# A table of planned starts, annealed with longer transfers in the plan, in place of the search in an attention and mixing kernel

## The chip, the cores and the metric

One core of one Trainium2 chip runs the whole program; the other cores are not used. The metric is the device time of one execution in microseconds, as the median over runs. The kernel before takes 596.05 us, the median of 3 runs (595.01 to 597.22).

## The reference

The reference is causal attention in a window of 128 positions with a linear bias, and a mixing block over its result:

```python
scores = scale * np.matmul(q, k.transpose(0, 1, 3, 2))
scores = np.where(mask, scores + bias[None], -1000000000.0)
attn = np.exp(scores - np.max(scores, axis=-1, keepdims=True))
attn = attn / (np.sum(attn, axis=-1, keepdims=True) + 1e-09)
x = np.matmul(attn, v)                      # 8 batches, 8 heads, 576 rows, 64 columns
theta = x @ w_theta                         # x as 8 x 576 x 512
zr, zi = x * np.cos(theta), x * np.sin(theta)
y = np.einsum('ts,bsd->btd', w_tok_r, zr) + np.einsum('ts,bsd->btd', w_tok_i, zi)
u = x + y
out = u + np.maximum(u @ w_ch, 0.0)
```

## The kernel before

Heads are taken in pairs, 4 pairs to a batch and 32 in all. For a pair, TensorE (PE) makes the scores in two groups (L624); VectorE (DVE) adds the band and takes the least value of each row (L648); ScalarE (ACT) makes the exponentials (L653). From pair 7 on ("late" pairs) the weights are split into two halves of 16 bits, the high one on ACT (L673) and the low one on DVE (L675), and are turned by a DMA transpose that SyncE (SP) issues (L679); the turned tiles are `pta` to `ptd`. PE then multiplies them with the values (L699 and L704, 72 matmuls for a pair: "attend"), and DVE divides by the sums (L712 to L716).

When the 4 pairs of a batch are there, the batch is turned, also by DMA transposes (L866, L867, L871), multiplied with the angle weights (L803, 12 matmuls a block; L808 and L812 for the short block), and made into `z_hi` and `z_lo` by way of the sine table (L826 to L845 and L420). Then PE mixes the tokens (L917): 8 results a batch, each of 27 matmuls of 288 columns, done in three parts of 9. DVE adds each result to `xtf` (L923), ACT and DVE split it (L927, L930), and PE does the channels (L951, 12 matmuls each); ACT, POOL or DVE finish, and SP stores (L970). The two banks `m_psa` and `m_psb` carry the results of L917 and L951 in turns, so that a bank is free for the next result only when DVE or ACT has read it. At the start, the three weight matrices are loaded in chunks (L432), and unpacked and split by DVE and ACT (L436 to L491), among the work on the first pairs.

Every step is first only recorded, with a cost (`Plan.__call__`): its engine, how long the engine is held, and a delay until its result can be used. A DMA is two steps, one on SP for the issue, and one on an engine called "DMA", which does one transfer at a time. `Plan.order` then sets the order: it simulates the plan backward and forward several times with greedy choices, keeps the best, and moves the keys of the steps by a fixed list of random numbers, `NUDGES`. `Plan.run` emits the steps in the order found, so that each engine's queue is in that order, and no engine passes a step by. Where the plan sees PE free, `run` puts filler matmuls of 187 columns on a tile of ones (L376, `spin`): one for each 0.085 of planned gap before 130, and one for each 0.085 of 0.8 of the gap after it.

Of the kernel before, what the change touches and what calls it, by code (L numbers as in the profile page):

```python
# [52 lines left out]
while RAD * 0.5 > math.pi:  # L53
# [11 lines left out]
TABLE = 1.3  # L65
HOLD = 12.0
RETILE = 0.11
STAY = 1.0
# [3 lines left out]
ROUNDS = 6  # L72
SELF = {"DVE": 0.115, "ACT": 0.13, "POOL": 0.1}
NUDGES = (
# [11 lines left out]
)  # L86
# [45 lines left out]
class Plan:  # L132
# [47 lines left out]
    def simulate(self, key, back):  # L180

        steps = self.steps
        engines = ("PE", "DVE", "ACT", "POOL", "SP", "DMA")
        free = dict.fromkeys(engines, 0.0)
        held = {"DVE": 0.0, "POOL": 0.0}
        open_ = {e: [] for e in engines}
        events, start = [], [0.0] * len(steps)
        wait = [len(s.after if back else s.deps) for s in steps]
        ready = [0.0] * len(steps)
        for s in steps:  # L190
            if not wait[s.n]:
                heapq.heappush(events, (0.0, s.n))
        table, now, order, tiled = None, 0.0, [], "f"
        into, out_of = (1, 0) if back else (0, 1)
        while len(order) < len(steps):
            while events and events[0][0] <= now + 1e-9:
                n = heapq.heappop(events)[1]
                heapq.heappush(open_[steps[n].engine], (key[n], n))
            for e in engines:
                if free[e] > now + 1e-9 or not open_[e]:  # L200
                    continue
                if e == "ACT":
                    extra = lambda t: TABLE if t.table not in (None, table) else 0.0
                    weight = HOLD / TABLE
                elif e == "PE":
                    extra = lambda t: RETILE if t.modes[into] != tiled else 0.0
                    weight = STAY / RETILE
                else:
                    other = {"DVE": "POOL", "POOL": "DVE"}.get(e)
                    extra = lambda t: max(0.0, held[other] - now) if t.port else 0.0  # L210
                    weight = 1.0
                if e == "DMA" and not back:
                    best = min(open_[e], key=lambda x: (ready[x[1]], x[1]))
                else:
                    best = min(open_[e], key=lambda x: (x[0] + weight * extra(steps[x[1]]), x[1]))
                open_[e].remove(best)
                heapq.heapify(open_[e])
                s = steps[best[1]]
                free[e] = now + s.busy + extra(s)
                table = s.table or table  # L220
                if e == "PE":
                    tiled = s.modes[out_of]
                if s.port:
                    held[e] = free[e]
                start[s.n] = free[e] - s.busy
                order.append(s)
                for a in (s.deps if back else s.after):
                    t = steps[a]
                    late = SELF.get(e, 0.0) if t.engine == e else t.late if back else s.late
                    wait[a] -= 1  # L230
                    ready[a] = max(ready[a], free[e] + late)
                    if not wait[a]:
                        heapq.heappush(events, (ready[a], a))
            if len(order) < len(steps) and not (events and events[0][0] <= now + 1e-9):
                now = min([t for t in free.values() if t > now + 1e-9] + [max(e[0], now) for e in events[:1]])
        end = max(free.values())
        if back:
            start = [end - t - s.busy for t, s in zip(start, steps)]
        return end, order, start

    def nudge(self, key, first, seed, span):

        state = seed

        def draw():
            nonlocal state
            state = (state * 6364136223846793005 + 1442695040888963407) & (1 << 64) - 1
            return (state >> 11) / (1 << 53)

        draw(), draw()  # L250
        size = 10.0 * draw()
        size *= draw()
        middle, about = draw() * span, 5.0 + draw() * 100.0
        sparse = draw() < 1.0 / 3.0
        out = []
        for k, t in zip(key, first):
            up, chance = draw(), draw()
            out.append(k + size * (2.0 * up - 1.0) if abs(t - middle) < about and (not sparse or chance < 0.2) else k)
        return out

    def order(self):
        steps = self.steps
        ahead = [0.0] * len(steps)
        for s in steps:
            ahead[s.n] = max((ahead[d] + steps[d].busy + steps[d].late for d in s.deps), default=0.0)
        key, best, span = [-(t + s.busy) for t, s in zip(ahead, steps)], None, 700.0
        for _ in range(ROUNDS):
            _, _, last = self.simulate(key, True)
            end, order, first = self.simulate(last, False)
            if best is None or end < best[0]:  # L270
                best = end, order, first, last
            key = [-(t + s.busy) for t, s in zip(first, steps)]
        end, order, first, last = best
# [7 lines left out]
        for s, t in zip(steps, first):  # L281
            s.start = t
# [19 lines left out]
def attn_moe_kernel(ctx: ExitStack, tc: tile.TileContext, qt, kt, vx, wth, wtok, wch, band, out):  # L302
    nc = tc.nc
# [800 lines left out]
```

## Time and profile before

| | |
|---|---|
| median of 3 runs | 596.05 us |
| the profiled execution | 594.92 us |
| its span, first to last instruction | 593.1 us |
| mean granted clock of TensorE | 0.994 |
| PE busy, fillers included | 580.1 us, 98% |
| fillers (L376), busy | 71.5 us in 556 |
| DVE, ACT, POOL busy | 493.1, 475.1, 157.1 us |

The span is what the trace covers; 1.8 us of the execution lie around it. PE counts as busy during its fillers, so its 98% has to be read together with them. A matmul's busy time is its passage through the engine, and matmuls overlap: 9 mixing matmuls follow each other in 1.10 us although each is shown with 0.29 us.

### The profile page before, as it was taken

Reading aid. Unit: us, or ns where it says so; the run is one execution under the profiler, and the core shown is the slowest. Engines: PE = TensorE matmul, PEld = TensorE weight load, DVE = VectorE, ACT = ScalarE, POOL = GpSimd, SP = SyncE. Lnnn points to the kernel's source line nnn. Section 1 sums busy time; section 2 is a strip of 40 time slices with the busy share of each in tenths; the row PEclk is TensorE's granted clock in tenths of the full one; section 3 lists DMA queues with packets and bytes.
Section 4 is the critical chain, followed back from the end, with each engine's and each line's share of the span. In section 5 each row is a group of like instructions: output and inputs, shape, how many; then the busy total and the mean of one; then the engine's idle time right before and its main releaser. Section 6 shows DMA issues by size and latency. Waiting matters only on the chain.

```text
span 593.1 us, 18474 instructions
## 1 busy us (share of the span) xinstructions
PE 580.1 (98%) x7524; PEld 442.8 (75%) x7524; DVE 493.1 (83%) x1523; ACT 475.1 (80%) x902; POOL 157.1 (26%) x135
## 2 busy tenths in 40 slices
PE   8999999999998999999999989999999999999997
PEld 8888876886676677776776757786767676777776
DVE  5999999999896998799879988878977989865333
ACT  4999999787999999999788978985998766446213
POOL 0000120011663106610573004700280127106000
PEclk9999999999998999999999989999999999999999
DMA  8975640897876964985469666438362613201102
GB/s 309 408 305 193 182 103 10 181 203 176 186 167 120 203 165 96 190 209 134 67 154 244 144 112 155 90 107 178 64 117 79 116 38 96 56 11 41 41 1 81
DMA packets 140102, 82.03 MB, mean 138 GB/s; under 512 B 119152, under 2 KB 127600, under 8 KB 140016
## 3 DMA queue, kind: packets, MB, share of 16 engines
q1 hardware_dynamic: 140016, 80.84, 56.4%
q8 instruction: 59, 0.97, 0.7%
q14 instruction: 27, 0.22, 0.1%
HBM read 42.29 MB, written 9.44 MB: 87 GB/s over the span
## 4 chain that ended last, share of the span: by engine, by line
PE 77%; ACT 8%; DVE 7%; DMA 4%; issue 2%; POOL 1%; SPq 0%; ACTq 0%; POOLq 0%
PE m_psa L917 15%; PE m_psb L917 15%; PE m_psa L951 8%; PE m_psb L951 7%; PE s_ps L624 7%; PE t_psa L803 6%; PE t_psb L803 5%; PE a_psa L376 3%; PE a_psa L704 2%; PE a_psb L376 2%; PE a_psb L704 2%; PE a_psa L699 1%; DMA xpa<-hlxa 1%; DMA ptc<-hla 1%; DMA ptb<-hlb 1%
## 5 line engine op out<-in xcount | busy, mean ns | idle before, releaser
L917 PEld LDWEIGHTS <-z_hi 128*128 128x128 f16 x1152 | 111.8, 98 | 31.9 <-issue 2.2
L951 PEld LDWEIGHTS <-wch 128*128 128x128 f16 x780 | 75.2, 98 | 19.2
L917 PE MATMUL m_psb<-wtk_hi,z_hi 128*128 128x288 f16 x288 | 83.1, 289 | 2.0 <-DVE xtfb L923 2.0
L917 PE MATMUL m_psb<-wtk_hi,z_lo 128*128 128x288 f16 x288 | 83.2, 289 | 0.0
L917 PE MATMUL m_psb<-wtk_lo,z_hi 128*128 128x288 f16 x288 | 83.1, 288 | 0.0
L917 PE MATMUL m_psa<-wtk_hi,z_hi 128*128 128x288 f16 x288 | 82.4, 286 | 0.0
L917 PE MATMUL m_psa<-wtk_hi,z_lo 128*128 128x288 f16 x288 | 82.4, 286 | 0.0
L917 PE MATMUL m_psa<-wtk_lo,z_hi 128*128 128x288 f16 x288 | 82.4, 286 | 0.0
L917 PEld LDWEIGHTS <-z_lo 128*128 128x128 f16 x576 | 56.6, 98 | 14.5
L420 POOL TENSOR_TENSOR z_lo<-wch_held,z_hi 128x512 f16<-128x512 f32 x32 | 40.7, 1285 | 87.0 <-ACT z_hi L845 52.2
L376 PEld LDWEIGHTS <-white 128*128 128x128 bf16 x556 | 48.9, 100 | 13.0 <-issue 5.9
L951 PE MATMUL m_psa<-u,wch 128*128 128x288 f16 (+1 forms) x396 | 53.2, 284 | 0.0
L376 PE MATMUL a_psa<-white 128*128 128x187 bf16 x418 | 50.0, 250 | 1.7 <-DVE a_psa L389 1.5
L951 PE MATMUL m_psb<-u,wch 128*128 128x288 f16 (+1 forms) x384 | 51.5, 284 | 0.0
L867 POOL TENSOR_TENSOR hlxa<-x_sba,hlxa 128x512 f16<-128x512 f32 (+1 forms) x12 | 16.2, 1347 | 111.0 <-ACT hlxa L866 111.0
L653 ACT ACTIVATE sba<-sba,fixed 128x192 f32<-128x192 f32 x88 | 36.3, 448 | 5.2 <-DVE fixed L648 4.5
L653 ACT ACTIVATE sbb<-sbb,fixed 128x192 f32<-128x192 f32 x84 | 34.7, 448 | 4.6 <-DVE fixed L648 4.6
L653 ACT ACTIVATE sbc<-sbc,fixed 128x192 f32<-128x192 f32 x84 | 34.7, 446 | 3.9 <-DVE fixed L648 3.9
L927 ACT ACTIVATE u<-xtfb,fixed 128x288 f16<-128x288 f32 x32 | 16.5, 527 | 24.5 <-DVE xtfb L923 24.5
L803 PEld LDWEIGHTS <-xpb 128*128 128x128 f16 x192 | 18.5, 98 | 21.4 <-DMA xpb<-hlxb 1.4
L803 PEld LDWEIGHTS <-xpa 128*128 128x128 f16 x192 | 18.4, 98 | 20.4 <-DMA xpa<-hlxa 1.1
L648 DVE CUSTOM_DVE_ANT_0 sbb<-s_ps,bands 128x192 f32<-128x192 f32 x84 | 26.5, 346 | 7.8 <-PE s_ps L624 7.7
(420 smaller groups left out, 1613.0 us busy)
## 6 DMA issues: line engine op xcount, KB each, us to landing
vba<-in_vx_dram SPq DMA_DIRECT2D x6, 845.0 KB, 6.3
out_dram<-xtfa SPq DMA_DIRECT2D x32, 144.0 KB, 1.9
out_dram<-xtfb SPq DMA_DIRECT2D x31, 144.0 KB, 1.8
vbb<-in_vx_dram SPq DMA_DIRECT2D x5, 845.0 KB, 5.4
vbc<-in_vx_dram SPq DMA_DIRECT2D x5, 845.0 KB, 5.8
qra<-in_qt_dram SPq DMA_DIRECT2D x11, 288.0 KB, 3.9
kra<-in_kt_dram SPq DMA_DIRECT2D x11, 288.0 KB, 3.8
krb<-in_kt_dram SPq DMA_DIRECT2D x11, 288.0 KB, 3.8
```

The lines of the kernel that those rows point to most:

```text
L376: nc.tensor.matmul(spun, white[:, :128], white[:, :spun.shape[-1]], start=True, stop=True)
L420: plan(engine, cost, lambda: on.tensor_tensor(out=out, in0=whole, in1=part, op=ALU.subtract), r=r, w=w, port=True)
L624: nc.tensor.matmul(ps.tile[at:at + 64, e, to:to + kn], qr.tile[rows, q0:q0 + 64], kr.tile[rows, k0:k0 + kn], start=True, stop=True)
L648: plan("DVE", (0.08 + kn * 1.03e-3, 0.13), lambda: nc.vector.tensor_tensor_reduce(out=out, in0=source, in1=bands[:out.shape[0], h, at:at + ...
L653: plan("ACT", (0.187 + kn * 0.833e-3, 0.15), lambda: nc.scalar.activation(out, source, AF.Exp, bias=least, scale=-1.0), r=r, w=w, table="exp")
L699: nc.tensor.matmul(av[e][cols, i, :d], block(c_, 1, a)[rows, cols], v[rows, slot, :d], start=c == 0 and k == 0, stop=False, skip_group_che ...
L704: nc.tensor.matmul(av[e][:, c + 1, :d], block(c, 2 * e, a), v[:, 4 * e + c, :d], start=False, stop=k == len(products) - 1, skip_group_chec ...
L803: nc.tensor.matmul(t_ps, a[:, c * 128:c * 128 + 128], w[:, c, :], start=(k == 0 and c == 0), stop=(k == len(prods) - 1 and c == 3))
L867: plan("POOL", pool(512), lambda: nc.gpsimd.tensor_tensor(out=lo, in0=x, in1=hi, op=ALU.subtract), r=every + [(hlx, "h")], w=[(hlx, "l")])
L917: nc.tensor.matmul(y.tile[:, :HALF], z[:, c, m * 128:m * 128 + 128], w[:, c, cs], start=(part == 0 and j == 0 and a == 0), stop=(part == 2 ...
L927: plan("ACT", (0.43, 0.15), lambda m=m, cs=cs, at=at: nc.scalar.activation(u_hi[:, m, cs], at, AF.Copy, scale=share), r=[(xtf, ("y", m, hf ...
L951: nc.tensor.matmul(o.tile[:, :n], w[:, c, e * 128:e * 128 + 128], u[:, c, cs], start=(k == 0), stop=(k == 11))
```

## The change

`Plan.order` no longer searches. It reads a table `STARTS`, one planned start in hundredths for every step in the order of recording, and sorts the steps by it. The simulation, the nudging and their constants are gone. `run` is as it was, and computes its fillers from the table's starts. Seven costs of transfers are changed; each is (SP held, "DMA" engine held, delay). The instructions that compute are the same, in number and in kind; their order on every engine is another, and there are 497 fillers for 556. Lines of the same statement lie 54 further down in the changed kernel: L376 becomes L430, L624 L678, L699 L753, L917 L971, L923 L977.

```diff
+STARTS = """
+    0 70 110 344 330 428 372 358 414 386 400 194 398 152 298 404 990 482 1426 1440 1931 2122 2196 2238 2314 2333
...
+    56501 56543 56583 56621 56479 56579 56621 56661 56697
+"""
...
     def order(self):
...
+        starts = [int(t) for t in STARTS.split()]
+        assert len(starts) == len(self.steps)
+        for s, t in zip(self.steps, starts):
+            s.start = t / 100.0
+        return sorted(self.steps, key=lambda s: (s.start, s.n))
...
-        issued.append(plan("SP", (0.42, w * 2.55e-3 + (0.7 if len(issued) < 3 else 0.0), 2.15),
+        issued.append(plan("SP", (0.42, w * 2.85e-3, 1.25),
...
-        plan.follow(plan("SP", (0.4, 0.75, 2.05), lambda: nc.sync.dma_start(
+        plan.follow(plan("SP", (0.42, 1.0, 1.2), lambda: nc.sync.dma_start(
...
-        values_issue[g] = plan("SP", (0.42, 2.05, 2.3), lambda: nc.sync.dma_start(
+        values_issue[g] = plan("SP", (0.36, 2.9, 1.6), lambda: nc.sync.dma_start(
...
-            plan("SP", (1.9, 2.0, 0.0), lambda hl=hl, turned=turned: nc.sync.dma_start_transpose(
+            plan("SP", (1.44, 2.0, 0.4), lambda hl=hl, turned=turned: nc.sync.dma_start_transpose(
...
-            plan("SP", (1.3, 1.4, 0.5) if wide else (1.2, 0.75, 0.65), lambda: nc.sync.dma_start_transpose(
+            plan("SP", (1.24, 1.42, 0.5) if wide else (1.2, 0.77, 0.55), lambda: nc.sync.dma_start_transpose(
...
-        plan("SP", (0.34, 0.45, 1.3), lambda: nc.sync.dma_start(
+        plan("SP", (0.36, 0.52, 1.2), lambda: nc.sync.dma_start(
```

The first place is PE at the end of batch 2 and the start of batch 3, where pair 12 attends (`pta` and `ptb` are its turned weights, `krc`, `qrc` the keys and queries of pair 14). Before:

```order
L917 MATMUL m_psb<-wtk_hi,z_lo 128x288
L376 LDWEIGHTS white
L376 MATMUL a_psb<-white 128x187
...
L624 MATMUL s_ps<-krc,qrc 64x64 x2
L376 LDWEIGHTS white
L376 MATMUL a_psb<-white 128x187
...
L699 LDWEIGHTS pta
L699 MATMUL a_psa<-vhb,pta 64x65
```

In the changed kernel, from the same scores on:

```order
L678 MATMUL s_ps<-krc,qrc 64x64 x2
L430 LDWEIGHTS white
L430 MATMUL a_psb<-white 128x187
L971 LDWEIGHTS z_hi
L971 MATMUL m_psa<-wtk_hi,z_hi 128x288
...
L678 MATMUL s_ps<-kra,qra 64x64 x2
L753 LDWEIGHTS pta
L753 MATMUL a_psa<-vhb,pta 64x65
```

Before, 5 fillers, a group of scores and 10 fillers stood directly ahead of the attend, and 17 and 5 more followed. Now one filler follows the scores, then 36 mixing matmuls, another group of scores, 24 angle matmuls and a third group of scores, and only then pair 12 attends.

The second place is DVE ahead of its first addition of a mixing result (L923, now L977), in batch 0. Before:

```order
L420 TENSOR_TENSOR z_lo<-fga,z_hi 128x512
L648 ISA firstb,fixed<-s_ps,bands 64x64
L648 ISA fixed 64x1
L675 SCALAR_TENSOR_TENSOR hlb<-sba,hlb 128x768
L582 TENSOR_TENSOR fixed<-fixed 128x1
...
L648 ISA sba,fixed<-s_ps,bands 128x192
L648 ISA fixed 128x1
L923 SCALAR_TENSOR_TENSOR xtfa<-m_psb,fixed,xtfa 128x288
L715 RECIPROCAL fixed<-fixed 128x5
L531 TENSOR_REDUCE fixed<-vbb 128x1
```

And in the changed kernel:

```order
L474 TENSOR_TENSOR z_lo<-wch_held,z_hi 128x512
L769 RECIPROCAL fixed<-fixed 128x5 x2
L652 TENSOR_SCALAR fixed<-fixed 128x1
L770 TENSOR_TENSOR x_sbb<-a_psb,fixed 128x5x64
L770 TENSOR_TENSOR x_sbb<-a_psa,fixed 128x5x64
L662 SCALAR_TENSOR_TENSOR vla<-vba,fixed,vha 128x832
L729 SCALAR_TENSOR_TENSOR hlb<-sba,hlb 128x768
L977 SCALAR_TENSOR_TENSOR xtfa<-m_psb,fixed,xtfa 128x288
L585 TENSOR_REDUCE fixed<-vbc 128x1
L702 ISA sba,fixed<-s_ps,bands 128x192
```

More pairs are divided and more values split or measured ahead of the first addition, and fewer scores. Counted from the start of the queue, the changed kernel has one L531, one L608, two L716 and eight small instructions more there (by the old lines), and three pairs of L648 fewer.

The third place is PE at pair 24, whose second group of scores is made from `kra` and `qra` and which attends with `pta` and `ptb`. In the changed kernel:

```order
L678 MATMUL s_ps<-kra,qra 64x128
...
L430 LDWEIGHTS white
L430 MATMUL a_psa<-white 128x187
...
L678 MATMUL s_ps<-krb,qrb 64x64 x2
L753 LDWEIGHTS ptc
L753 MATMUL a_psa<-vha,ptc 64x65
...
L753 LDWEIGHTS pta
L753 MATMUL a_psa<-vhb,pta 64x65
```

Between these scores and pair 24's attend now stand 81 mixing matmuls, two groups of scores, one attend and five fillers; before, more than four times that work stood between them.

## Rows read from the trace of the kernel before

**Rows 1.** The page: span, and busy time, share and instructions of each engine.

```profile
span 593.1 us, 18474 instructions
PE 580.1 (98%) x7524; PEld 442.8 (75%) x7524; DVE 493.1 (83%) x1523; ACT 475.1 (80%) x902; POOL 157.1 (26%) x135
```

**Rows 2.** Fillers alone (L376) by stretches: us, PE busy, PEld busy, clock, DMA share, GB/s.

```profile
0.00:100.00 100.00, 44.44 (x421) 35.81 (x422) 1.00 0.65 224
...
172.00:186.00 14.00, 5.49 (x42) 4.11 (x41) 0.88 0.82 142
...
sum 593.10, PE 71.48 PEld 48.86; mean PE 8.94 PEld 6.11
```

**Rows 3.** All engines in the same stretches: PE, PEld, DVE, ACT, POOL busy, clock, DMA.

```profile
172.00:186.00 14.00, 11.77 (x212) 10.03 (x211) 9.92 (x42) 13.96 (x26) 7.92 (x7) 0.88 0.82 142
...
349.00:356.00 7.00, 4.96 (x26) 2.71 (x24) 6.92 (x28) 6.50 (x11) 0.00 (x0) 0.76 0.43 45
...
416.00:593.10 177.10, 173.60 (x1772) 130.34 (x1764) 122.14 (x291) 104.16 (x187) 48.33 (x37) 1.00 0.26 62
```

**Rows 4.** Timeline around pair 12: PE, DVE and SP, start us, us, what.

```profile
166.50 0.90 PE L624 MATMUL s_ps<-kra,qra 64*64 64x128 f32 x24
167.21 0.19 PE L699 MATMUL a_psa<-vha,ptc 64*64 64x65 f16 x1
...
168.48 0.19 PE L704 MATMUL a_psb<-vha,ptd 128*128 128x65 f16 x1
...
177.16 0.98 PE L376 MATMUL a_psb<-white 128*128 128x187 bf16 x10
...
173.14 0.92 DVE L675 SCALAR_TENSOR_TENSOR hlb<-sbb,hlb 128x768 f16<-128x768 f32 x1
...
173.89 0.42 SPq L503 DMA_DIRECT2D krb<-in_kt_dram  x1
```

**Rows 5.** The chain that ended last, in order of time: transfers, and one part of a mixing result.

```profile
106.90 1.10 PE m_psb L917 x9
...
174.41 6.11 DMA ptb<-hlb
```

**Rows 6.** A filler alone between steps, PE.

```profile
169.61 0.24 PE L376 MATMUL a_psa<-white 128*128 128x187 bf16 x1
169.78 0.99 PE L624 MATMUL s_ps<-krb,qrb 64*64 64x64 f32 x30
170.71 0.26 PE L376 MATMUL a_psa<-white 128*128 128x187 bf16 x1
170.81 0.29 PE L917 MATMUL m_psa<-wtk_hi,z_hi 128*128 128x288 f16 x1
```

**Rows 7.** All engines at the start and in batch 0.

```profile
25.00:50.00 25.00, 24.25 (x422) 21.77 (x421) 24.67 (x117) 24.85 (x59) 0.00 (x0) 1.00 0.80 301
...
100.00:125.00 25.00, 24.21 (x362) 20.38 (x360) 24.76 (x97) 20.42 (x45) 0.00 (x0) 1.00 0.83 163
```

**Rows 8.** Timeline of DVE and PE: the first addition of a mixing result, a value split.

```profile
107.35 0.35 DVE L648 CUSTOM_DVE_ANT_0 sba<-s_ps,bands 128x192 f32<-128x192 f32 x1
...
107.62 0.08 DVE L648 DVE_READ_ACCUMULATOR2_ANT fixed<- 128x1 f32 x1
...
108.10 0.52 DVE L923 SCALAR_TENSOR_TENSOR xtfa<-m_psb,fixed,xtfa 128x288 f32<-128x288 f32 x1
...
108.62 1.32 DVE L531 TENSOR_REDUCE fixed<-vbb 128x1 f32<-128x1152 f32 x1
109.86 0.48 DVE L716 TENSOR_TENSOR x_sbb<-a_psa,fixed 128x320 f32<-128x320 f32 x1
...
108.94 0.29 PE L917 MATMUL m_psb<-wtk_hi,z_hi 128*128 128x288 f16 x1
...
188.94 1.08 DVE L608 SCALAR_TENSOR_TENSOR vlb<-vbb,fixed,vhb 128x832 f16<-128x832 f32 x1
```

**Rows 9.** Timeline of PE at its longest late wait on DVE.

```profile
352.22 0.28 PE L917 MATMUL m_psb<-wtk_hi,z_hi 128*128 128x288 f16 x1 [2.04 <-DVE xtfb L923]
```

More of the change, by code (lines that the diff above doesn't have):

```diff
@@ L1 @@
 from contextlib import ExitStack
-import heapq
 import math
@@ L62 @@
 COLUMNS = (1, 2, 3, 4, 0)
[L65 to L68, printed above, removed]
 SPIN = 0.085
@@ L71 @@
 FIRST = 2.0
-ROUNDS = 6
-SELF = {"DVE": 0.115, "ACT": 0.13, "POOL": 0.1}
-NUDGES = (
[11 rows of a table removed]
-)
+STARTS = """
[169 rows of a table added]
+"""
 def dve(n, two=False):
@@ L178, in follow @@
         other.after.append(s.n)
[L180 to L259, printed above, removed]
@@ L261, in order @@
-    def order(self):
[L262 to L273, printed above, removed]
-        for seed in NUDGES:
-            last = self.nudge(last, first, abs(seed), span)
-            end, order, first = self.simulate(last, False)
-            if seed < 0:
-                _, _, last = self.simulate([-(t + s.busy) for t, s in zip(first, steps)], True)
-                end, order, first = self.simulate(last, False)
-        self.end = end
-        for s, t in zip(steps, first):
-            s.start = t
-        return order
+    def order(self):
+        starts = [int(t) for t in STARTS.split()]
[3 more added lines that the diff above has]
+        return sorted(self.steps, key=lambda s: (s.start, s.n))
@@ L500, in load_pair @@
         qr, kr = qr_ring.take(), kr_ring.take()
-        plan.follow(plan("SP", (0.4, 0.75, 2.05), lambda: nc.sync.dma_start(
+        plan.follow(plan("SP", (0.42, 1.0, 1.2), lambda: nc.sync.dma_start(
             out=qr.tile, in_=qt[b, h:h + 2].rearrange("h d s -> (h d) s")), w=[(qr, 0)]), begin)
-        plan.follow(plan("SP", (0.4, 0.75, 2.05), lambda: nc.sync.dma_start(
+        plan.follow(plan("SP", (0.42, 1.0, 1.2), lambda: nc.sync.dma_start(
             out=kr.tile, in_=kt[b, h:h + 2].rearrange("h d s -> (h d) s")), w=[(kr, 0)]), begin)
```

178 rows, old and new, of tables (NUDGES, STARTS) are left out of this document.

## The prediction

> **What bounds the kernel now.** I read the page first. PE is busy for 580.1 of 593.1 us and no other engine for more than 493.1 [rows 1], so time can only be won where PE does no work of the task: while it idles (13.0 us), and in its fillers. A reader has to take the fillers out of the 98%: they are 556 matmuls with 71.48 us of busy time [rows 2], so that PE works for about 508.6 us, and some 84.5 us of the span are waits, filled or bare. The second view is therefore the fillers by stretches, in the same group, and beside it all engines in the same stretches [rows 3]. Of the fillers' time 44.44 us lie in the first 100 us, where the weights are unpacked. There DVE sets the pace: it is busy for 24.67 of 25 us, and still for 24.76 of 25 in the first mixing batch [rows 7]. Later the fillers are few, except in one place, 172 to 186 us, with 42 of them. From 416 us on PE is busy for 173.60 of 177.10 us, and the 3.5 us that are left are about the tail behind its last matmul. So the end is set by PE's work, plus the waits of the start, plus the few waits between 100 and 416 us.
>
> The third view is the timeline around the place with the 42 fillers [rows 4]. The second group of pair 12's scores ends at 167.4 us (166.50 and 0.90). DVE begins the low half of these weights at 173.14, SP puts a load of keys into the queue at 173.89, and the transpose goes out at 174.41 and lands 6.11 us later [rows 5], at 180.5. PE reached the attend after 10 fillers at 178.1, and waited in the middle of it. Of the 14 us PE idles 2.23 (14.00 less 11.77) and spends 5.49 on fillers, so 7.7 us are no work of the task [rows 2, 3]. This includes what the clock took: 0.88 of full over 14 us is a loss of 1.7 us, in stretches at 1.2 instead of 2.4 GHz after PE had idled.
>
> **The change, part by part.**
>
> The seven costs of transfers change nothing by themselves: no DMA gets larger or faster. They only stand behind the table. Dropping the search costs nothing on the chip, as it ran when the kernel was built. What acts is the order, and the number of fillers, 497 for 556.
>
> *Pair 12 attends later.* In the order before, PE has some 8 us of its own work between the second scores of pair 12 and its attend: four mixing parts of 1.10 us [rows 5], another attend of 1.3 us (167.21 to 168.5, [rows 4]), and three groups of scores of 0.7 to 0.9 us ([rows 4, 6]). The weights needed 13.1 us (167.4 to 180.5). In the new order the attend stands behind some 28 us of work, and 3 fillers are left in the same stretch of PE's work where 39 were by the count of the order. I take the 7.7 us as gone, but for three fillers of 0.1 us: **-7.4 us**. The bounds are 0, if another engine can't keep up when PE no longer waits, and -7.7. What speaks against the 0 is ACT, which is full in this stretch (13.96 of 14.00, [rows 3]): counted in the order, with the mean durations of its lines, it has 9 us less work ahead of the first split of batch 1 (L927, the ninth in its queue) than before, and DVE has 8 us less ahead of the same addition (L923), while PE stands at the same amount of work to within 1 us. What is late next there is the mixing itself, which PE then does without a wait.
>
> *Single fillers.* Behind this place the new order has 51 fillers for 66, and between the start and it two more, so 13 fewer, nearly all of them alone between two steps. One alone delays the scores behind it by 0.17 us from its start, and the mixing behind it by 0.10 (169.61 to 169.78, and 170.71 to 170.81, [rows 6]). Some of this stays as the change between tile shapes, so I take the smaller: **-1.3 us**, between 0 and -2.2 (13 by 0.17).
>
> *The start and batch 0.* Up to the end of the first six mixing parts PE has 10 fillers fewer; they only cover waits there and are taken at nothing. If the wait that they cover is bare instead, it is as long. DVE is the engine to ask, and its queue is longer now ahead of the first addition: one L531 (1.24 us to the next start, [rows 8]), one L608 (1.08, 1.0 to the next start, same rows), two L716 (0.48, and 0.4 to the next start) and eight small ones of some 0.1, less three L648 of 0.27 to the next (107.35 to 107.62): 3.0 us. PE has 0.6 us more of its work ahead of the same result. Ahead of the eighth addition DVE has 7.1 us more and PE 4.5. The next result needs the bank that this addition frees, so PE waits for the difference, less what slack there is: at the first addition the bank is free at 108.6 (108.10 and 0.52) and PE takes it at 108.94 [rows 8], so 2.4 less 0.3, and 2.6 at the eighth. These are the same wait and not two. I take **+2.0 us**, between -1.5 and +2.6. The lower bound would be gained at the very start: the second pair's keys and queries now come ahead of the third chunk of weights, and DVE's short waits before 15 us may shrink.
>
> *SP's queue.* In the early part the loads change places with each other, and the third and fourth chunk of the first weights have fewer bytes ahead of them than before, by one load of values less two loads of a pair, and then by one load of values. From batch 1 on the transposes stand behind one load or two, as they did. I cost this at nothing, because 20 us and more of PE's work lie between scores and attend for most late pairs, and the two exceptions are a rival below.
>
> *Other late waits.* The largest is at 350 us: PE idles 2.04 us for an addition of DVE's [rows 9], and the clock of that stretch is 0.76 over 7 us, 1.7 us lost [rows 3]: 3.7 us in all. It belongs to an order that is gone; I expect a wait of the same kind and size somewhere in the new one, so 0, between -3.7 and +3.7.
>
> The sum is -7.4 - 1.3 + 2.0 = -6.7 us on the profiled execution: 594.92 becomes 588.2. That execution was 1.13 us below the median of 596.05, so I predict a median of **589.4 us**.
>
> The trace shows the clock at 1.00 over the first 100 us with their 421 fillers, and lower in the two stretches that hold more than 2 us of bare idle time [rows 2, 3]. The Trainium skill (TensorE: Matmul & The Clock Gate, "Why this matters for your kernels") says that PE should have no idle gaps of a few microseconds between bursts of matmuls, or else its clock is halved; that speaks against taking fillers out. By the trace the fillers that go are those of a wait that goes; by the rule alone they would each be a risk, and the sum would be the one of the second rival.
>
> **The rivals.**
>
> 1. *The waits of two tight pairs.* In the new order, pair 24 has 12.9 us of PE's work between scores and attend: 81 matmuls of 0.122 us [rows 5], two groups of scores (0.9 and 0.7), an attend of 1.3. Pair 27 has about 17.2. If the low half comes as fast as for pair 12 and the transpose lands as late (6.11, [rows 5]), pair 24 needs the same 13.1 us; and for pair 27 DVE has 11.6 us queued from the first score to the low half, which with 6.5 us until landing makes 18.1. The waits are then 0.2 and 0.9 us, and if each also brings a fall of the clock, 1.7 each: +4.5, and 593.9 us. For it speaks that the one late transpose of before cost PE 7.7 us; against it that a wait so short need not lower the clock.
> 2. *Bare waits lower the clock.* With fewer fillers in the start and the late part, waits that the table does not foresee stay bare. Each fall costs 1.7 us as at 172 and 349 us [rows 3]; four of them take the gain away: 596.2 us. Against it: only two such stretches are in the trace of before, with 84 us of waits.
> 3. *A dense order has no slack for late additions.* This is the wait at 350 us [rows 9], where L923 was late in DVE's queue and held a bank. It costs 3.7 us each time. The table packs the steps closely, and there are seven more batches in which it can happen; with three more than before the gain is gone and the kernel is slower by 0.7%, with four it takes 604.2 us. For it speaks that DVE is nearly full until 125 us; against it that DVE has work ahead of the additions that is 2 to 23 us less than before from the ninth to the 56th.
> 4. *The unforeseen waits go too.* The 3.7 us at 350 us vanish and DVE's start costs nothing: 6.7 + 3.7 + 2.0 = 12.4 us less, 583.7 us.
>
> **How the numbers follow.** A measurement of this kernel can tell about 0.5%, 3 us, from no change. My forecast has 0.55, with a range of its own from 586 to 593; rival 1 0.14, rival 2 0.06, rival 3 0.12, rival 4 0.13. Faster by over 0.5% are the forecast and rival 4: 0.68. Within 0.5% are rivals 1 and 2: 0.20. Slower is rival 3: 0.12. The range from 582 to 598 takes in rival 4 and its bounds (a single filler's 0.17), rivals 1 and 2, and the mildest form of rival 3; its stronger forms, about 0.1, are left out.
>
> **What would show it.** Right: no stretch after 170 us with more than a few fillers, PE's clock at 1.00 from 172 to 186, and PE busy for some 573 us of a span near 586; the first additions at 110 to 112 us; fillers' busy time down by about 7 us. Wrong: idle time of PE at the attend of pairs 24 or 27 released by DMA (rival 1), slices of the clock below 1.00 in new places (rival 2), or waits of L971 on DVE's L977 in several batches (rival 3). If DVE is not busy between 25 and 125 us, the third term is wrong.

## The result, and the profile after

The changed kernel takes 586.71 us (median of 4 runs, 585.55 to 587.92), the kernel before beside it 596.48 us (595.01 to 597.22): a ratio of 0.984 with a 95% interval of 0.981 to 0.987. In a second comparison, on the same chip as three of the experiments, it took 587.21 us for 595.88, a ratio of 0.986 (0.984 to 0.988). The forecast was 589.4 us. The profiled execution took 585.89 us, 9.03 less than that of before, where the sum of the terms was 6.7.

The page of the changed kernel answers to [rows 1]; beside it stands the row of the clock in 40 slices:

```profile
span 584.1 us, 18356 instructions
PE 574.0 (98%) x7465; PEld 436.5 (75%) x7465; DVE 488.9 (84%) x1523; ACT 480.1 (82%) x904; POOL 158.5 (27%) x135
...
PEclk9999999999999999999999999999999999999999
```

All engines by stretches, the changed kernel ([rows 3, 7] before): PE, PEld, DVE, ACT, POOL busy, clock, DMA share, GB/s.

```profile
100.00:125.00 25.00, 22.62 (x345) 18.80 (x343) 22.78 (x85) 21.34 (x46) 0.00 (x0) 1.00 0.73 158
...
172.00:186.00 14.00, 14.00 (x240) 11.31 (x237) 12.64 (x51) 13.47 (x31) 7.72 (x6) 1.00 0.79 179
...
349.00:356.00 7.00, 7.00 (x112) 5.77 (x100) 6.46 (x21) 6.42 (x13) 1.31 (x2) 1.00 0.39 128
```

Its fillers (now L430) by the same stretches ([rows 2] before): PE busy, clock, DMA share, GB/s.

```profile
0.00:100.00 100.00, 44.47 (x410) 1.00 0.67 224
...
172.00:186.00 14.00, 0.80 (x4) 1.00 0.79 179
...
sum 584.10, PE 63.68; mean PE 9.10
```

The 14 us after 172 are full of PE's own work but for 0.80 us of four fillers, and the clock is 1.00 there and at 349 us. The fillers of the first 100 us are as before (44.47 for 44.44 us). DVE, which had 24.76 of 25 us in 100 to 125, now has 22.78: something holds it up there.

Where the time went is best read from **PE's lag**: the start of one of its matmuls, less the time that its own matmuls ahead of it (without fillers) take at the spacing at which they follow each other in the trace at full clock (0.1225 us in a mixing part, 0.216 in an angle, and so on; 513.4 us in all). The lag grows only where PE waits, runs fillers or runs slowly. In us, at seven amounts of PE's own work, one profiled execution each:

```
own work done           60    100    120    160    260    280    500
before                59.3   59.1   66.8   67.8   70.4   74.1   77.3
changed               62.4   63.1   63.8   64.7   65.9   66.2   68.4
changed, once more    63.7   64.4   65.0   67.2   68.9   69.2   71.3
e1_costs              75.1   75.9   86.4   87.7   97.0   99.8  105.8
e2_loads              60.5   60.3   66.7   67.7   69.3   72.6   76.3
e8_attend_later       60.4   60.2   69.9   75.4   78.6   82.7   88.3
e7_before_bare        64.1   63.6   70.7   71.7   75.9   77.7   80.7
h1_new_then_old       62.5   63.3   64.0   65.2   73.9   76.1   81.6
h2_old_then_new       61.3   61.1   69.8   70.1   72.9   73.5   76.5
e3_values             60.3   61.3   62.0   62.8   63.8   64.0   65.8
e4_bare               62.7   62.9   63.0   63.3   64.2   64.8   65.6
e6_both               61.0   61.5   61.6   61.7   62.3   62.8   63.3
e10_earlier           62.4   64.1   64.2   64.9   67.7   68.3   69.2
e5_none               69.1   69.0   69.1   70.6   73.1   74.2   74.5
```

Two executions of the changed kernel differ by up to 3 us along this table, so a difference of 1 us in it says little, and a jump at one place more. From before to the changed kernel, to the nearest tenth: up to 110 us of own work it lags 63.5 for 58.7, 4.8 us **lost**; over the stall of pair 12 (110 to 120) 0.3 are added for 8.1, 7.8 **won**; from there to the end 4.6 for 10.5, 5.9 **won**, 3.4 of them between 260 and 280, where the wait of [rows 9] was.

What is lost early has one large piece. Timeline of the changed kernel, SP, ACT, DVE and PE (in brackets the idle time before and who ended it):

```profile
105.51 0.33 SPq L563 DMA_DIRECT2D vbc<-in_vx_dram  x1
105.89 1.63 SPq L733 DMA_TRANSPOSE ptc<-hla  x1
...
113.95 0.84 ACT L727 ACTIVATE hla<-sbb 128x768 f16<-128x768 f32 x1 [2.33 <-DMA ptc<-hla]
...
114.83 0.96 DVE L729 SCALAR_TENSOR_TENSOR hla<-sbb,hla 128x768 f16<-128x768 f32 x1 [1.88 <-ACT hla L727]
...
116.72 0.24 PE L430 MATMUL a_psa<-white 128*128 128x187 bf16 x1 [1.99 <-DVE fixed L766]
116.89 0.90 PE L678 MATMUL s_ps<-kra,qra 64*64 64x128 f32 x24
```

A load of values (845 KB) goes out directly ahead of the first late transpose. The transposes' row of that stretch says that it landed 8.0 us after its issue:

```profile
ptc<-hla SPq DMA_TRANSPOSE x1, 8.0
```

ACT may not write the next high half into `hla` before that, DVE waits for ACT, its divisions (L766) and minima (L702) stand behind, and PE idles 1.99 us ahead of its scores. The table itself has this transpose land 5.3 us after its issue (issue at 102.93 in the plan, transfer from 105.83, 2.0 and 0.4 us), so the plan is 2.7 us short here and leaves no room for the rest.

### The profile page after: what moved, and what is told of

Same layout as the page of the kernel before. It is cut to its first block, busy times and chain, and to the rows that moved or that the text cites. A ratio compares the mean times of both kernels' runs of the same rounds, so it can differ in the third digit from the quotient of the medians.

```text
span 584.1 us, 18356 instructions
## 1 busy us (share of the span) xinstructions
PE 574.0 (98%) x7465; PEld 436.5 (75%) x7465; DVE 488.9 (84%) x1523; ACT 480.1 (82%) x904; POOL 158.5 (27%) x135
## 4 chain that ended last, share of the span: by engine, by line
PE 62%; ACT 10%; DMA 7%; DVE 4%; issue 2%; POOL 1%; SPq 0%; DVEq 0%; ACTq 0%; POOLq 0%
PE m_psa L971 13%; PE m_psb L971 13%; PE m_psa L1005 7%; PE m_psb L1005 7%; PE t_psa L857 5%; PE s_ps L678 5%; PE t_psb L857 4%; DMA xpb<-hlxb 2%; DMA xpa<-hlxa 1%; PE a_psa L758 1%; DMA ptc<-hla 1%; PE a_psb L758 1%; DMA ptd<-hlb 1%; PE a_psa L430 1%; PE t_psb L862 1%
## 5 line engine op out<-in xcount | busy, mean ns | idle before, releaser
L971 PEld LDWEIGHTS <-z_hi 128*128 128x128 f16 x1152 | 111.4, 98 | 29.9 <-issue 0.9
L971 PE MATMUL m_psb<-wtk_hi,z_hi 128*128 128x288 f16 x288 | 82.4, 286 | 0.8 <-DVE fixed L627 0.8
L971 PE MATMUL m_psa<-wtk_hi,z_hi 128*128 128x288 f16 x288 | 82.4, 286 | 0.0
L971 PE MATMUL m_psa<-wtk_hi,z_lo 128*128 128x288 f16 x288 | 82.4, 286 | 0.0
L971 PE MATMUL m_psa<-wtk_lo,z_hi 128*128 128x288 f16 x288 | 82.4, 286 | 0.0
L971 PE MATMUL m_psb<-wtk_hi,z_lo 128*128 128x288 f16 x288 | 82.4, 286 | 0.0
L971 PE MATMUL m_psb<-wtk_lo,z_hi 128*128 128x288 f16 x288 | 82.4, 286 | 0.0
L971 PEld LDWEIGHTS <-z_lo 128*128 128x128 f16 x576 | 56.4, 98 | 14.2
L430 PE MATMUL a_psa<-white 128*128 128x187 bf16 x412 | 49.4, 254 | 4.0 <-DVE fixed L766 2.0
L430 PEld LDWEIGHTS <-white 128*128 128x128 bf16 x497 | 44.1, 101 | 11.8 <-issue 4.7
L921 POOL TENSOR_TENSOR hlxb<-x_sbb,hlxb 128x512 f16<-128x512 f32 (+1 forms) x12 | 15.5, 1288 | 94.7 <-ACT hlxb L920 94.7
L921 POOL TENSOR_TENSOR hlxb<-x_sba,hlxb 128x512 f16<-128x512 f32 x8 | 11.1, 1381 | 80.5 <-ACT hlxb L920 80.4
```

The lines of the kernel that those rows point to most:

```text
L430: nc.tensor.matmul(spun, white[:, :128], white[:, :spun.shape[-1]], start=True, stop=True)
L921: plan("POOL", pool(512), lambda: nc.gpsimd.tensor_tensor(out=lo, in0=x, in1=hi, op=ALU.subtract), r=every + [(hlx, "h")], w=[(hlx, "l")])
L971: nc.tensor.matmul(y.tile[:, :HALF], z[:, c, m * 128:m * 128 + 128], w[:, c, cs], start=(part == 0 and j == 0 and a == 0), stop=(part == 2 ...
```

## The experiments

The theory: PE's late waits come from transposes that land late, and an order that knows when they land has neither the waits nor the filled time; single fillers cost little. The rivals: the attend's place alone decides; the loads ahead of the transposes alone decide; the fillers keep the clock. Edits that move steps name a step and the one that it then stands behind on its engine; the order on each engine is otherwise kept, and so are the fillers ahead of each step. In these kernels lines stand later than in their base: by 30 in those that move or drop something, by 18 and 19 in the two joined orders (against before).

**The costs alone (e1_costs).**

```diff
-        plan.follow(plan("SP", (0.4, 0.75, 2.05), lambda: nc.sync.dma_start(
+        plan.follow(plan("SP", (0.42, 1.0, 1.2), lambda: nc.sync.dma_start(
...
-            plan("SP", (1.9, 2.0, 0.0), lambda hl=hl, turned=turned: nc.sync.dma_start_transpose(
+            plan("SP", (1.44, 2.0, 0.4), lambda hl=hl, turned=turned: nc.sync.dma_start_transpose(
```

> The kernel before, its search and its seeds, with the seven new costs of transfers alone. Theory A (the new costs by themselves bring the gain, as any search that knows them leaves transposes more room): 588 to 592 us, no stall of several us around pair 12. Theory B (what acts is the order that the table holds; the old search, whose 105 seeds were drawn for the other costs, finds no such order): the order that it makes ends in its own plan at 602.7 us where the order before ends at 573.0, and holds 828 fillers for 556, so some 25 to 30 us slower than before, 615 to 630 us.

Measured: 622.62 us, ratio 1.044 (1.040 to 1.048). Its lag is already 16 us larger when 60 us of work are done, and the stall of pair 12 is still there (75.9 to 86.4). Knowing the costs is not what wins; the order is. What a new search with seeds of its own would find with these costs was not tried.

**Loads behind the transposes, in the order before (e2_loads).**

```diff
+MOVES = ((2493, 2098), (2128, 1910), (1388, 1061), (1390, 1388))
```

> The kernel before, where three loads that stand directly ahead of a transpose in SP's queue go directly behind it (the values before the transposes at 315 and 338 us, the keys and queries of a pair before the one at 174 us); nothing else moves. Theory A (PE's late waits come from transposes that land late because a load goes ahead of them): the waits at 322 us (0.9) and 350 us (2.04 and 1.7 of clock) go, and 1.5 to 2.5 of the 7.7 us around pair 12: 590 to 592 us. Theory B (the waits are set by the queues of DVE and ACT, the loads ahead of a transpose are hidden): 595 to 597.5 us.

Measured: 596.10 us, ratio 0.9995 (0.997 to 1.002): no change. The profile says why. The transpose of pair 12 now lands 3.7 us after its issue for 6.11 [rows 5], and no attend waits for a DMA. But PE now waits longer elsewhere, for the transposes ahead of the angles above all (L833 here, L803 before):

```profile
PE t_psb L833 <- DMA xpa<-hlxa: 2.4, 1, 2.4
PE t_psb L833 <- DMA xpb<-hlxb: 1.8, 1, 1.8
...
PE s_ps L654 <- DVE fixed L678: 0.9, 1, 0.9
...
PE m_psb L947 <- DVE xtfb L953: 0.6, 1, 0.6
```

The first of these stands at 185.8 us, right behind pair 12: over the stall the lag grows by 6.4 us instead of 7.7. The second, at 405 us, was 1.1 us before. The wait of [rows 9] is down to 0.6 us (last line) and the one at 322 us is gone, but 0.9 us at 332 and 0.7 at 334 us are new. Theory A was right about each transpose and wrong about the time.

**Pair 12's attend alone later (e8_attend_later).**

```diff
+MOVES = ((1295, 1349), (1296, 1290), (1299, 1296), (1380, 1337))
```

> The kernel before, where pair 12's attend alone goes later: behind the second scores of pair 14, an angle (L803) and the first scores of pair 15, 4.1 us more of PE's own work by the plan's durations; on DVE its two L712 go behind the low half of pair 13 and the low half of pair 14's values (L612 by the plan) behind that of pair 13, as they must. Theory A (the forecast's: the stall of 7.7 us is the wait of this attend, and the work ahead of it in PE's queue decides it): 3 to 4 us less, 592 to 593 us. Theory B (DVE, ACT and the transposes behind it are late as well, there is no other work ready for PE; the attend's place alone wins nothing, and what follows from it comes later): 596 to 602 us.

Measured: 603.73 us, ratio 1.012 (1.007 to 1.016). PE by its waits from 176 to 200 us, and all engines over the two stretches:

```profile
181.03 0.90 PE L654 MATMUL s_ps<-krc,qrc 64*64 64x128 f32 x24 [1.17 <-DVE fixed L678]
184.47 1.89 PE L833 MATMUL t_psb<-wth_hi,xpa 128*128 128x512 f16 x4 [2.04 <-DMA xpa<-hlxa]
194.99 0.30 PE L947 MATMUL m_psb<-wtk_hi,z_hi 128*128 128x288 f16 x1 [0.77 <-ACT z_hi L875]
196.61 0.30 PE L947 MATMUL m_psb<-wtk_hi,z_lo 128*128 128x288 f16 x1 [1.20 <-POOL z_lo L450]
```

```profile
172.00:186.00 14.00, 10.66 (x142) 7.94 (x141) 12.17 (x56) 12.14 (x25) 7.93 (x6) 0.92 1.05 168
186.00:200.00 14.00, 12.02 (x145) 6.83 (x144) 4.54 (x8) 6.53 (x13) 2.66 (x2) 0.74 0.43 119
```

The attend does not wait any more, but everything that PE could do in its place does: scores for DVE, an angle for its transpose, mixing parts for ACT and POOL, and DVE then has 4.54 of 14 us of work, as pair 14's values and the divisions wait for the attend. The time lies above both ranges, and the profiled execution is the slowest of the four (606.03 us). Three steps of DVE had to move with the attend, so the edit is not its place alone; together with e2, where no attend waits for a DMA and the time stays, it says that the stall was not the wait of one instruction.

**New start with the old rest, old start with the new rest (h1, h2).** The list of steps is joined from the two orders, each piece with its own fillers; a step goes into the first piece if both orders have it early.

```diff
-        for s in self.order():
+        for s in (self.steps[n] for n in line):
+            if s.n in fill:
+                spin(tiles[fill[s.n][0]], fill[s.n][1])
...
```

> The changed kernel's order for all steps up to about 169 us of PE's work (the start, batch 0 and pair 12's attend with its surroundings), and from there the order before, with the fillers of each. Theory A (the stall of pair 12 is won in full, but the start gives some of it back, and about 6 us are won later on, in many small places, as the sums of PE's lost time by its work say: 65.0 for 67.9 us at this point, then 9.4 us to the end before for 3.4 after): 2.9 us less than before, 592 to 594 us, with up to 3 more where the two orders meet. Theory B (the forecast's own account: all of the gain but 1.3 us lies at pair 12 and in the start): 590 to 591 us.

> The order before for all steps up to about 139 us of PE's work (the start, batch 0 and the stall around pair 12), and from there the changed kernel's, with the fillers of each. Theory A (67.1 us lost at this point, then 4.6 to the end for 10.2 before): 5.6 us less than before, 589.5 to 591.5 us, with up to 3 more where the two orders meet. Theory B (the later part gives only single fillers, 1.3 us): 594 to 595.5 us.

Measured: 598.37 us, ratio 1.005 (1.002 to 1.008), and 594.11 us, ratio 0.997 (0.995 to 0.999). The totals decide little (h1 lies above both of its ranges, h2 lies within theory B's and, with the cost of joining, within theory A's), since joining cost more than was allowed for: in h1 the lag jumps from 65.2 to 71.1 where the pieces meet, with waits of 1.2 and 1.8 us for DVE at 227 and 231 us. The pieces themselves say more. With the new start the stall of pair 12 is gone (63.3 to 64.0). With the old rest its late waits are back, for the same releasers as in the kernel before (there at 322, 352 and 406 us):

```profile
325.92 1.04 PE L822 MATMUL t_psb<-wth_hi,xpa 128*128 128x512 f16 x4 [0.69 <-DMA xpa<-hlxa]
...
354.99 0.28 PE L936 MATMUL m_psb<-wtk_hi,z_hi 128*128 128x288 f16 x1 [1.33 <-DVE xtfb L942]
...
408.32 1.04 PE L822 MATMUL t_psb<-wth_hi,xpb 128*128 128x512 f16 x4 [2.10 <-DMA xpb<-hlxb]
```

With the new rest (h2) the lag grows by 6.9 us from 140 us of work on, against 10.2 before, and 4.6 and 6.3 in the two traces of the changed kernel. So the late waits belong to the old order's late part and do not come back in the new one.

**The load of values behind the late transpose, in the changed kernel (e3_values).**

```diff
+MOVES = ((650, 629), (653, 606))
```

> The changed kernel, where the load of values that stands directly ahead of the first late transpose (105.5 us) goes directly behind it, and DVE's L585 that reads these values goes behind a multiplication of L770 some 5 us later; nothing else moves. Theory A (the wait of 1.99 us at 116.7 us comes from this transpose, which took 8.0 us to land: ACT waited 2.3 us for it, then DVE 1.9 us for ACT, then PE for DVE): that chain of waits goes, 584 to 585 us. Theory B (DVE is the bound up to 125 us and the wait only changes its name): 586 to 587.5 us.

Measured: 585.96 us, ratio 0.982 (0.979 to 0.985), beside 0.984 and 0.986 for the changed kernel. The transpose lands after 3.7 us instead of 8.0, ACT no longer waits for it, and the scores start at 114.44 instead of 116.89 us:

```profile
ptc<-hla SPq DMA_TRANSPOSE x1, 3.7
```

```profile
114.44 0.90 PE L708 MATMUL s_ps<-kra,qra 64*64 64x128 f32 x24
```

In the trace 2.1 us of lag are gone at 60 us of work, and 2.6 at the end. Its runs spread from 583.32 to 587.23, so alone it is within what a comparison here can tell. The landings are no chance of one execution: 7.8 to 8.0 us in the four profiles with the load ahead (the changed kernel's two, e4 and h1), 3.7 in the three with it behind (e3, e6, e10). The Trainium skill (DMA: Bandwidth & Descriptors, "Two DMAs through the same engine are not ordered") says that the descriptors within one queue of a DMA engine start in order; these landings agree with it.

**The changed kernel without its late fillers (e4_bare).**

```diff
+def KEPT(s):
+    return s.start < FULL
...
-                spin(tiles[k], int(share * (s.start - max(last, used[k])) / SPIN))
+            if s.engine == "PE" and KEPT(s):
+                spin(tiles[fill[s.n][0]], fill[s.n][1])
```

> The changed kernel without the 66 fillers behind 130 us of the plan, 61 of them alone between two steps. Theory A (a filler alone costs the step behind it 0.10 us, the price that the prediction took): 66 by 0.1, 579.5 to 581 us. Theory B (a filler alone sits in a gap that is there anyway, at a wait or a change of tile shape): 585 to 587.5 us. Theory C (bare waits lower the clock): stretches behind 130 us with a granted clock under 1.00, 1.7 us for each, 588 to 592 us.

Measured: 584.68 us, ratio 0.981 (0.977 to 0.985). From 60 us of work to the end the lag grows by 2.9 us instead of 6.0: 3.1 us for 66 fillers, **0.05 us each**, half of theory A's price (4.7 us and 0.07 each against the changed kernel's second trace). No slice of the clock falls. Part of what the fillers covered is bare now:

```profile
PE t_psb L887 <- DMA xpa<-hlxa: 1.2, 2, 0.7
PE t_psa L887 <- DMA xpa<-hlxa: 0.9, 1, 0.9
PE m_psb L1035 <- DVE xtfa L1007: 0.6, 1, 0.6
```

**Both edits, and the comparison run (e6_both, after_again).**

> The changed kernel with the load of values behind the late transpose of 105.5 us, L585 later, and without the 66 fillers behind 130 us of the plan: both edits at once. Theory A (each saves what the traces show, 2.3 us at 116.7 us and 3.1 us of fillers, and they add up): 581 to 582.5 us. Theory B (one takes the other's slack, new waits for transposes take the place of the fillers): 584 to 586 us.

> The changed kernel as it is, once more, beside the next three on one chip: 585.5 to 588 us by every theory.

Measured on one chip: 582.26 us, ratio 0.977 (0.975 to 0.980), beside 587.21 us for the changed kernel. The two savings add up (4.95 us between the medians, 5.1 us of lag in the first profile), and this version is faster than both kernels. Each edit can be read from it alone as well: against e4 the moves give 2.4 us, against e3 the fillers 3.7 (between medians on two chips; 2.1 and 2.7 by the ratios).

**The kernel before without its late fillers (e7_before_bare).** The same edit as e4, in the kernel before.

> The kernel before without its 118 fillers behind 130 us of the plan, 42 of them in the stall of pair 12. Theory A (a filler alone costs 0.05 us net, as the changed kernel without its 66 showed, and those in the stall cost nothing): some 70 by 0.05, 3 to 4 us less, 592 to 593.5 us. Theory B (the bare wait of some 8 us at pair 12 lowers the clock for longer): a granted clock under 0.9 from 172 to 190 us, and 596 to 600 us.

Measured: 594.51 us, ratio 0.997 (0.994 to 0.999), between the two. The stall is bare now, with 2.27 us at the attend for the transpose, and the clock is low for longer: before it is 0.88 from 172 to 186 us [rows 3] and 1.00 after that, here

```profile
172.00:186.00 14.00, 9.68 (x216) 7.65 (x207) 12.41 (x53) 13.99 (x29) 9.37 (x8) 0.93 0.66 164
186.00:200.00 14.00, 13.63 (x132) 8.84 (x130) 12.10 (x38) 13.13 (x27) 2.28 (x3) 0.83 0.85 199
```

This profiled execution is the slowest of the twelve (598.16 us). It also lost nearly 5 us before 60 us of work that the kernel before does not lose, with the same fillers there. Most of it stands at 73.6 us: a transpose of `xpa` landed 6.0 us after its issue, 3.7 in the kernel before, PE waited bare for 2.05 us, and the granted clock is 0.72 from 73 to 79 us. Why it landed later in this execution, the runs don't settle.

**Fewer fillers early, and none (e10_earlier, e5_none).** The first is e6 with another bound; in the second no filler is kept, and nothing is moved.

```diff
-    return s.start < FULL
+    return s.start < 90.0
```

> As the run with both edits at once (load of values behind the transpose, L585 later, no fillers behind 130 us of the plan), but the fillers go from 90 us of the plan on: 75 more, nearly all in waits of the last weights. Theory A (fillers in a wait cost nothing but the end of the last one, and the one that stands on the bank that DVE still reads, 0.4 us): 0 to 1 us less than that run, 581 to 582.5 us. Theory B (three bare waits of 1.3 to 2.7 us in a row lower the clock): a granted clock under 0.9 between 95 and 110 us and 584 to 587 us.

> The changed kernel without any filler. Theory A (the fillers keep the clock up in the first 100 us, where PE waits for DVE for some 50 us): a granted clock well under 1.00 in the first 100 us; what PE does of its own work there then takes up to twice as long, but DVE sets the pace, so no more than 5 us are lost: 584 to 592 us. Theory B (PE's own work there lies in the path of DVE's, and the clock falls again and again): over 595 us. Theory C (the clock does not fall, and the fillers only delay): 575 to 582 us.

Measured: 588.39 us, ratio 0.986 (0.983 to 0.990), some 6 us over the run with both edits, which ran on another chip (7.7 and 13.6 us under the kernel before beside each), and above both ranges; and 591.99 us (one run), in theory A's range. Without the fillers from 90 us of the plan on, PE waits bare for 2.70 us, and the granted clock falls to half, the lower of its two levels, until about 109 us (PE, PEld, DVE, ACT, POOL busy, clock, DMA share, GB/s):

```profile
96.00:98.00 2.00, 0.76 (x6) 0.46 (x4) 2.00 (x6) 2.00 (x4) 0.00 (x0) 1.00 0.00 0
98.00:100.00 2.00, 0.17 (x1) 0.10 (x1) 2.00 (x7) 1.99 (x5) 0.00 (x0) 0.65 0.00 0
100.00:102.00 2.00, 2.00 (x9) 1.03 (x7) 2.00 (x10) 2.00 (x4) 0.00 (x0) 0.50 0.00 0
```

With both edits and these fillers the clock is 1.00 there. So the fillers in this stretch are worth what they cost, and those alone between steps are not.

## Why the prediction was right, and where it was not

**Pair 12** (-7.4 forecast, -7.8 found). The size was right, and the place: 14.00 of 14.00 us busy, clock 1.00. The mechanism was told too simply. "The attend stands behind some 28 us of work" is not enough: e8 moved it behind more work, with three steps of DVE, and lost 7.7 us, e2 brought its transpose in time and won nothing. What the forecast counted beside it, that ACT and DVE have 8 to 9 us less ahead of the first addition of batch 1, seems to belong to the cause: in e8 and e2 PE waits next for other operands (minima, an angle's transpose, `z`), so these have to come in time as well. h1 shows that the order up to there does this by itself; which of its many moves are needed was not taken apart.

**Single fillers** (-1.3). The price of 0.10 us was read as a delay in the trace; removed, 66 of them give 0.05 each. For 13 that is -0.6.

**The start and batch 0** (+2.0, bound +2.6; found +4.8). This is the step that failed in its mechanism: "its queue is longer now ahead of the first addition", said of DVE. The first addition did come late, at 110.4 us, as forecast, but without the transpose's wait (e3) PE lags only 1.0 us more than before at 60 us of work. By the forecast's own test the term is wrong, since DVE idles 2.2 of the 25 us from 100 on. What costs some 2 us (2.1 of lag in e3) is in the term that was set at nothing, **"SP's queue"**: the forecast argued that 20 us of PE's work lie between scores and attend, so that a transpose behind a load is hidden. It looked only at who reads the transposed weights. A transpose also holds its source `hla`, one of two buffers, and the next writer of that, on ACT, is no 20 us away. e3 and e6 removed this piece. The other 2.7 us are spread: 1.0 ahead of it, 1.7 between 60 and 110 us of work, and their cause stays open; without the late fillers (e4, e6) the lag grows by only 0.2 to 0.5 us from 60 to 100 us of work, with them by 0.7.

**Other late waits** (0 forecast, within 3.7 both ways; with the fillers -5.9 found, so outside the bound). "I expect a wait of the same kind and size somewhere in the new one" was wrong: in the changed kernel's first profile the only late wait of PE over 0.5 us is 0.8 us for DVE, in its second one 1.5 us for an angle's transpose, 0.9 and 0.6 us. The old waits were read as chance of a dense order, but each has a transpose behind it. At 322 and 406 us PE waits for one itself, and ahead of the wait of [rows 9] stands the chain that the changed kernel has at 113 us. Timeline of the kernel before, ACT and DVE:

```profile
344.86 0.84 ACT L673 ACTIVATE hla<-sba 128x768 f16<-128x768 f32 x1 [2.30 <-DMA ptc<-hla]
...
345.74 0.96 DVE L675 SCALAR_TENSOR_TENSOR hla<-sba,hla 128x768 f16<-128x768 f32 x1 [2.10 <-ACT hla L673]
```

e2 moved the load ahead of that transpose behind it: it landed after 4.0 us instead of 6.4, and the wait fell from 2.04 to 0.56 us. h1 and h2 show that these waits belong to the old late part. That the new order avoids them since its plan holds the "DMA" engine longer for loads would fit this, but the plan was 2.7 us short at the transpose of 105.9 us, and e1 shows only that the costs without the order don't do it; an order annealed with the old costs was not tried.

**The rivals.** Rival 1: no attend of pairs 24 or 27 waits. Rival 2 in small: in the first profile the clock stays up, but in the second one it falls once, right behind the wait at 116 us,

```profile
117.00:120.00 3.00, 3.00 (x35) 1.84 (x29) 3.00 (x14) 3.00 (x9) 0.00 (x0) 0.59 1.02 180
```

and its lag at 60 us of work is 1.3 us larger. It fits that five of the changed kernel's nine runs and three of e4's six, which all have this wait, show a mean clock of 0.996 or 0.997, and none of the eleven runs of e3 and e6, which lack it, is under 0.999. No fall came from the fillers that went later, nor without any late ones (e4); the Trainium skill's rule that was weighed against taking fillers out (TensorE: Matmul & The Clock Gate, "Why this matters for your kernels") agrees with e10 and e7, where bare waits of 2.70 us and of 2.05 to 2.36 us went with falls of the clock, and speaks for no filler that stands alone. The length of a wait alone does not tell: the clock stayed at 1.00 behind 1.99 us in the first profile and 2.37 us in e2, and fell behind 1.89 us in the second profile. Rival 3: no L971 waits on L977 for more than 0.5 us. Rival 4 was half right: the late waits went, the start cost more. So the sum, -6.7 for -9.0 in the profiled executions, came near by luck as well: +2.8 in the start and -4.6 later partly cancel (-7.8 + 4.8 - 5.9 = -8.9).

## What to carry to other kernels

When a transfer is moved, ask who reads what it brings and also who waits to write what it reads: here a ring of two source buffers put some 2 us on PE through ACT and DVE, and one load moved behind the transpose, with the step of DVE that reads it, took them off again. A stall of the bounding engine need not be one instruction's wait; move that instruction alone, and if the wait only changes its name, the engines behind it are late too. Fillers were worth some 6 us in the stretch with the wait of 2.70 us, and those behind 130 us of the plan, nearly all alone between steps, cost about 0.05 us each: take them out by groups and look at the clock of the stretch.

## What was unexpected in the hardware

Without any filler the first scores run at not much over half their pace, though the row of the granted clock says 1.00. PE's timeline at the first scores of pairs 0 and 1, without fillers and then in the changed kernel, and between them the stretch of the run without fillers (the clock is the third number from the end):

```profile
7.61 1.76 PE L708 MATMUL s_ps<-kra,qra 64*64 64x64 f32 x30 [7.61 <-DMA qra<-in_qt_dram]
...
13.89 1.76 PE L708 MATMUL s_ps<-krb,qrb 64*64 64x64 f32 x30 [0.16 <-DVE fixed L732]
...
17.27 1.56 PE L708 MATMUL s_ps<-krb,qrb 64*64 64x128 f32 x24 [0.79 <-DVE fixed L732]
...
34.25 0.90 PE L708 MATMUL s_ps<-krc,qrc 64*64 64x128 f32 x24 [0.25 <-DVE fixed L732]
```

```profile
0.00:25.00 25.00, 14.81 (x168) 11.39 (x168) 17.10 (x75) 15.64 (x36) 0.82 (x8) 1.00 0.93 353
```

```profile
8.05 0.99 PE L678 MATMUL s_ps<-kra,qra 64*64 64x64 f32 x30
...
13.22 0.99 PE L678 MATMUL s_ps<-krb,qrb 64*64 64x64 f32 x30
```

The same 30 matmuls take 1.76 us for 0.99, and from 34 us on they are at full pace (24 in 0.90 us, 1.56 at 17 us) without a change in that row (1.00 for 0 to 25 us). What the trace holds of the clock begins only with a rise to full, at 31.20 us in this run (6.49 in the changed kernel), and the row counts the time before that as 1.00. So the row shows the falls later in the run, as at 98 us above, but not the slow beginning: there the mean duration of a matmul is the better clock. The Trainium skill (TensorE: Matmul & The Clock Gate, "Seeing it yourself") says that the clock's events in a trace were seen to be unreliable; in this run the events that are recorded agree with the durations, and only what lies before the first one is missing.

A second thing is how much a load ahead of it adds to a transpose: the same transpose of 12 blocks took 8.0 us directly behind 845 KB, and 3.7 us ahead of them. Behind smaller loads it differs from one execution to the next: the transpose of `xpa` at 67 us, behind two loads of 288 KB, landed after 3.7, 4.0, 5.5 and 6.0 us in the kernel before, e8, h2 and e7, which issue these three transfers in the same order.
